# Packed attention and a two-layer mixer on one core: the packed values as twenty small matmuls instead of five wide ones

## The chip, the core and the metric

The kernel runs on one core of a Trainium2 chip. The core has a matrix engine (TensorE, PE; its weight loads are listed apart as PEld), three engines for elementwise work (VectorE or DVE, ScalarE or ACT, GpSimd or POOL), a sync engine (SyncE, SP) that only issues transfers here, and 16 DMA engines that move data between the device memory and the on-chip memory. Matrix products land in PSUM, a small accumulator memory of 128 partitions, and are read from there by DVE or ACT.

The metric is device microseconds from the first to the last instruction of one execution, as the runs report it. Lower is better. Before the change three runs gave 883.6, 884.82 and 885.3 us; the median is 884.82 us.

## The reference, cut to what matters

```python
# batch 8, heads 8, seq 576, head_dim 64, 32 packs; q, k, v, p in float32
def sm_attn(qq, kk, vv):
    s = scale * np.matmul(qq, kk.transpose(0, 1, 3, 2))
    s = s - np.max(s, axis=-1, keepdims=True)
    a = np.exp(s)
    a = a / (np.sum(a, axis=-1, keepdims=True) + 1e-09)
    return np.matmul(a, vv)
p_packed = sm_attn(p, k, v)                  # per batch and head: [32, 64]
x = sm_attn(q, p_packed, p_packed)           # heads side by side: [8, 576, 512]
h = x.transpose(0, 2, 1) @ U @ V             # mixes tokens, rank 32
u = x + h.transpose(0, 2, 1)
out = u + np.maximum(u @ w_ch1, 0.0) @ w_ch2 # 512 -> 2048 -> 512
```

U, V, w_ch1 and w_ch2 arrive as float64 and are made float32 on the chip.

## The kernel before, in words

The work has two phases. Phase A makes the packed values `pp` of every batch, which is `p_packed` of the reference, and the product `pp w1` for the first four batches. Phase B computes, batch by batch, the two large products, while the attention of the next batches and `pp w1` of the later ones are made beside it.

In phase A the unit of work is four heads of one batch: 16 units, u = 0 to 15. A unit goes through these steps. `a_load` and `a_load_v` bring k and v. `a_split` transposes k on DVE (tile `kT`, one instruction at line 106). `a_scores` makes the scores of the 4 x 32 packs against 576 tokens on PE (line 331), so that partition 32 h + n of the tile `s_ps` is pack n of head h. `a_softmax` takes the row maximum on DVE (line 339, tile `mx`) and the exponential on ACT (line 341). `a_turn` transposes the exponentials back on PE (lines 351 and 352) and copies them on ACT into `eT`, five blocks of up to 128 tokens, the last of 64. `a_pack` multiplies them with v (lines 367 and 368, tile `pp_ps`) and scales the result on ACT into `ppall` (line 371). `a_pairs` transposes pairs of heads for the product with w1.

In `a_pack` before the change the left operand is a block of `eT` with all four heads' 32 packs as its 128 columns, and the right operand is v of all four heads, 4 x 64 columns. The product therefore holds every head's packs against every head's values, 128 x 256, of which the four blocks on the diagonal are used. Each block is read by a copy of its own, 32 partitions by 64.

Between the units phase A converts w1, 16 chunks of 128 x 512. One conversion is a square on ACT (line 67), four instructions on DVE (lines 68, 69, 70 and 76), a rounding copy on ACT (line 128, tile `w1h`) and a subtraction on POOL (line 129, tile `w1l`). `fold(r, pr)` multiplies the transposed packed values of round r (two batches) with the four chunks of row block pr of w1 (tile `w_ps`, three buffers; three matmuls a chunk, lines 81 to 83), copies each chunk's product to a tile `fold` (six buffers; line 401 on ACT, and in round 1 line 399 on DVE for every second chunk) and writes it to device memory (line 402, target `wsr`). The folds take their `fold` tiles in the order of the program, all of round 0 before round 1, so the 16 folds of round 1 come after the one that needs the last chunk of w1. `load_wt` reads the first columns back (line 450), and line 461 on ACT with line 462 on POOL splits them into the tile `wt`, the first weights of phase B.

The attention of batch 0 runs within phase A too, in small steps. Its last ones, which I call the attention's tail, are `tokens` (PE transposes, line 236 on ACT, three subtractions into `tl` at line 237 on DVE), `mix1` (15 matmuls into `m_ps`, line 246 on ACT, two subtractions into `ms` at line 249 on DVE) and `mix2` (four matmuls, four additions into `aT` at line 259 on DVE, line 260 on ACT, line 261 on POOL).

The order in which phase A's instructions stand on each engine isn't that of the source. A scheduler sets it when the program is built: it takes the dependences and its own estimate of every instruction's length, and places what can run. If an instruction is said to be shorter, the order of everything around it can change, on all engines and in the DMA queue of SP. An engine then executes its instructions strictly in that fixed order, and waits where an operand is late. Phase B is in an order written out by hand.

Of the kernel before, what the change touches and what calls it, by code (L numbers as in the profile page):

```python
# [8 lines left out]
F32 = mybir.dt.float32  # L9
# [10 lines left out]
def packed_attention_mixer_kernel(  # L20
# [11 lines left out]
):  # L32
    """x = packed attention, u = x + (x^T U V)^T, out = u + relu(u w1) w2.

    The attention output has rank 32 per head: x = A pp with A [tokens, (head, pack)].  So
    u = A' pp with A' = A + (A^T U V)^T, and u w1 = A' (pp w1).  Phase A makes pp of every batch and
    pp w1 of the first half of them; phase B does the rest of each batch while A' of the next one and
    pp w1 of the later ones are made.

    The large products are of float32r: an operand is the exact sum of two such parts (hi, lo), a  # L40
    product is hi*hi + hi*lo + lo*hi.  U, V, w1 and w2 come as the bits of float64 and are made
    float32 on the chip, to all 24 bits.
    """
    nc = tc.nc
    B, H, S, D = q.shape
# [11 lines left out]
    HALF = ((0, 256), (256, 320))  # L57
    # the float32 with the bits of the high word of the float64 2^-126
    LEAST = 1.125 * 2.0 ** -15
# [3 lines left out]
    def float32_of(x, t, raw, pool):  # L63
        """x (int32 words) = float32 bits of the float64s in raw [..., 2]; t is as large.  A float64
        below float32's normal range becomes zero, on GpSimd if pool."""
        low, high = raw[:, :, 0], raw[:, :, 1]
# [27 lines left out]
    nc.gpsimd.memset(bdq, 0.0)  # L94
    # pp w1: rows (pair of heads, batch of a round, head, pack) of the first batches, (head, pack) of the others
    wsr = [dram.tile([2 * H * NP, DF], F32, name=f"wsr{r}", tag=f"wsr{r}") for r in range(2)]
    wsc = {b: dram.tile([H * NP, DF], F32, name=f"wsc{b}", tag=f"wsc{b}") for b in range(B // 2, B)}

# [1 line left out]
    def load_nat(pool, bufs, src, b, g):  # L100
# [10 lines left out]

# [1 line left out]
    def weight_tiles(name):  # L113
# [16 lines left out]

# [1 line left out]
    uh = const.tile([P, 5, 4, R], F32R, name="uh")  # L132
# [31 lines left out]

# [1 line left out]
    def attention(b, res):  # L166
        """Steps that leave A'^T of batch b, in hi and lo parts, in res."""
        st = {}
# [114 lines left out]

    # ================= phase A: packed keys and values, and pp w1 of the first batches =================
    actx = ExitStack()
# [75 lines left out]
    def a_pack(u):  # L361
        b, g = UN[u]
        eT, vt, rs = ua[u]["eT"], ua[u]["v"], ua[u]["sum"]
        pp_ps = psA.tile([P, 4, D], F32, name="pp_ps", bufs=1)
        vm = vt[:, :4].rearrange("p h x -> p (h x)").rearrange("p (h k d) -> p k h d", h=4, k=4)
        for kk in range(4):
            nc.tensor.matmul(pp_ps, lhsT=eT[:, kk], rhs=vm[:, kk], start=kk == 0, stop=False)
        nc.tensor.matmul(pp_ps, lhsT=eT[:64, 4], rhs=vt[:64, 4].rearrange("p (h d) -> p h d", h=4), start=False, stop=True)
        for h in range(4):
            hs = slice(32 * h, 32 * h + 32)  # L370
            nc.scalar.activation(ppall[hs, b, g], pp_ps[hs, h], AF.Copy, scale=rs[hs])
        if b < B // 2:
            ua[u]["twice"] = sA.tile([P, 2, D], F32, name="twice", bufs=1)
            nc.scalar.copy(ua[u]["twice"], ppall[:, b, g].unsqueeze(1).to_broadcast([P, 2, D]))

    def a_pairs(u):
        """pp^T, block diagonal over the heads of a pair, for the two batches of a round"""
        b, g = UN[u]
# [11 lines left out]
    def fold(r, pr):  # L390
        """rows of pp w1 of a pair of heads, of both batches of round r"""
        wh, wl = w1t[pr]
# [145 lines left out]

    # ================= phase B =================
    ctx.enter_context(tc.manual_schedule())  # L540
# [17 lines left out]

# [1 line left out]
    def later(pr):  # L560
# [50 lines left out]
    class Batch:  # L611
# [8 lines left out]
        def blocks(self):  # L620
            """pp, block diagonal over the heads of a group, and the columns of A' left for the joint tile"""
            for h in range(4):
# [54 lines left out]
    def joint(b):  # L677
        """the last 64 tokens of batches b - 1 and b"""
        oj = psO.tile([P, DM], F32, name="o", tag="o")
        for kt in range(NK):  # L680
            kj = jslot(b, kt)
            mm3(oj, (hjh[:, kj], hjl[:, kj]), w2_parts(kt), kt == 0, kt == NK - 1)
            if kt == 0:
                for i in range(2):
                    residual(oj, ajh[i], ajl[i], rdh[i], rdl[i])
        return oj
# [107 lines left out]
```

## Time and profile before

| | |
|---|---|
| median of three runs | 884.82 us (883.6 to 885.3) |
| profiled execution, first to last instruction | 882.5 us |
| PE busy | 830.5 us, 94% |
| DVE busy | 538.2 us, 61% |
| ACT busy | 374.7 us, 42% |
| POOL busy | 317.7 us, 36% |
| copies of `pp_ps` on ACT, line 371 | 64, 19.5 us |
| matmul passes into `pp_ps`, lines 367 and 368 | 160 |

The profiled execution has a time of its own, 882.5 us between its first and its last instruction; what a run reports beyond that lies around the span. Shares over the whole span hide that the two phases are bound by different engines; a table by stretches of time shows it. In the lists below, a line number is that of the kernel before; "out<-in" names the tiles; "x8" is a count of merged instructions; a bracket behind a row is the idle time before it and what ended it. A float32 matmul is listed as two passes, each with its weight load. The end of a pass is modelled, so the distance between the starts of two passes says more than the length of one.

### The profile page before, as it was taken

Reading aid. Unit: us, or ns where it says so; the run is one execution under the profiler, and the core shown is the slowest. Engines: PE = TensorE matmul, PEld = TensorE weight load, DVE = VectorE, ACT = ScalarE, POOL = GpSimd, SP = SyncE. Lnnn points to the kernel's source line nnn. Section 1 sums busy time; section 2 is a strip of 40 time slices with the busy share of each in tenths; the row PEclk is TensorE's granted clock in tenths of the full one; section 3 lists DMA queues with packets and bytes.
Section 4 is the critical chain, followed back from the end, with each engine's and each line's share of the span. In section 5 each row is a group of like instructions: output and inputs, shape, how many; then the busy total and the mean of one; then the engine's idle time right before and its main releaser. Section 6 shows DMA issues by size and latency. Waiting matters only on the chain.

```text
span 882.5 us, 12689 instructions
## 1 busy us (share of the span) xinstructions
PE 830.5 (94%) x4480; PEld 708.8 (80%) x4480; DVE 538.2 (61%) x1023; ACT 374.7 (42%) x960; POOL 317.7 (36%) x268
## 2 busy tenths in 40 slices
PE   4889788878989999999999999999999999999997
PEld 3556566767879888898889888988898889889886
DVE  7999997989957876478676343444543524432220
ACT  2556567634444555455554233223333322333220
POOL 3322344745346545255454232323232313221110
PEclk9999899999999999999999999999999999999999
DMA  9879657723424444334452203010301120002001
GB/s 315 239 241 289 208 174 256 256 79 103 157 63 121 130 141 124 113 102 120 128 166 87 65 13 111 25 43 34 111 25 56 55 76 25 25 13 93 28 1 59
DMA packets 59998, 98.55 MB, mean 112 GB/s; under 512 B 12192, under 2 KB 36768, under 8 KB 59936
## 3 DMA queue, kind: packets, MB, share of 16 engines
q1 hardware_dynamic: 59936, 97.75, 35.2%
q8 instruction: 35, 0.57, 0.3%
q14 instruction: 27, 0.22, 0.1%
HBM read 71.52 MB, written 26.21 MB: 111 GB/s over the span
## 4 chain that ended last, share of the span: by engine, by line
PE 68%; DVE 21%; issue 4%; POOL 2%; DMA 2%; ACT 2%; SPq 0%; DVEq 0%; ACTq 0%
PE o L83 14%; PE o L81 13%; PE o L82 13%; PE h_ps L81 7%; PE h_ps L82 6%; PE h_ps L83 6%; DVE os L69 3%; DVE kT L106 3%; DVE os L70 2%; DVE natT L106 2%; DVE os L76 2%; DVE os L68 2%; PE w_ps L601 2%; DVE hl L649 1%; PE t_ps L234 1%
## 5 line engine op out<-in xcount | busy, mean ns | idle before, releaser
L649 DVE SCALAR_TENSOR_TENSOR hl<-h_ps,hh 128x256 fp32r<-128x256 f32 x256 | 104.1, 418 | 180.8 <-ACT hh L647 145.0
L83 PE MATMUL o<-w2h,hl 128*128 128x512 f32 x512 | 202.0, 395 | 0.0
L81 PE MATMUL o<-w2h,hh 128*128 128x512 f32 x512 | 201.1, 393 | 0.0
L82 PE MATMUL o<-w2l,hh 128*128 128x512 f32 x512 | 200.7, 392 | 0.0
L647 ACT ACTIVATE hh<-h_ps 128x256 fp32r<-128x256 f32 x256 | 96.0, 384 | 231.4 <-PE h_ps L83 228.4
L462 POOL TENSOR_TENSOR fold<-fold 128x512 fp32r<-128x512 f32 x62 | 83.6, 1349 | 217.2 <-ACT fold L461 216.5
L81 PE MATMUL h_ps<-ah,fold 128*128 128x256 f32 x496 | 149.4, 301 | 10.2 <-DVE hl L649 9.8
L82 PE MATMUL h_ps<-al,fold 128*128 128x256 f32 x496 | 146.3, 295 | 0.0
L83 PE MATMUL h_ps<-ah,fold 128*128 128x256 f32 x496 | 145.7, 294 | 0.0
L83 PEld LDWEIGHTS o<-w2h,hl 128*128 128x128 f32 x512 | 96.3, 188 | 21.4
L82 PEld LDWEIGHTS o<-w2l,hh 128*128 128x128 f32 x512 | 96.5, 189 | 17.6
L81 PEld LDWEIGHTS o<-w2h,hh 128*128 128x128 f32 x512 | 96.4, 188 | 16.8
L81 PEld LDWEIGHTS h_ps<-ah,fold 128*128 128x128 f32 x496 | 93.4, 188 | 17.8 <-DVE hl L649 14.6
L82 PEld LDWEIGHTS h_ps<-al,fold 128*128 128x128 f32 x496 | 93.5, 189 | 2.2
L83 PEld LDWEIGHTS h_ps<-ah,fold 128*128 128x128 f32 x496 | 93.5, 188 | 0.0
L190 POOL TENSOR_TENSOR nlo<-natT,nhi 128x576 fp32r<-128x576 f32 x32 | 46.7, 1476 | 106.9 <-ACT nhi L189 106.9
L69 DVE SCALAR_TENSOR_TENSOR os<-bits,os 128x512 int32<-128x512 int32 x48 | 55.9, 1164 | 1.3
L331 PE MATMUL s_ps<-kT,bdp 128*128 128x288 f32 x128 | 42.4, 485 | 10.7 <-DVE bdp L322 8.9
L70 DVE SCALAR_TENSOR_TENSOR os<-bits,os 128x512 int32<-128x512 int32 x48 | 45.2, 943 | 1.5
L331 PEld LDWEIGHTS s_ps<-kT,bdp 128*128 128x128 f32 x128 | 28.4, 230 | 20.0 <-issue 8.9
L189 ACT CAST nhi<-natT 128x576 fp32r<-128x576 f32 x32 | 20.7, 674 | 54.7 <-DVE natT L106 52.0
L129 POOL TENSOR_TENSOR w1l<-os,w1h 128x512 fp32r<-128x512 f32 x16 | 21.9, 1366 | 57.6 <-ACT w1h L128 57.6
(148 smaller groups left out, 1472.3 us busy)
## 6 DMA issues: line engine op xcount, KB each, us to landing
bits<-in_moe_w_ch_dram SPq DMA_DIRECT2D x48, 512.0 KB, 4.2
nat<-in_k_dram SPq DMA_DIRECT2D x16, 576.0 KB, 4.9
nat<-in_q_dram SPq DMA_DIRECT2D x16, 576.0 KB, 4.4
vt<-in_v_dram SPq DMA_DIRECT2D x16, 512.0 KB, 5.8
wsr<-fold SPq DMA_DIRECT2D x32, 256.0 KB, 4.3
out_dram<-bits SPq DMA_DIRECT2D x16, 512.0 KB, 3.0
wsc<-bits SPq DMA_DIRECT2D x64, 128.0 KB, 2.2
fold<-wsc SPq DMA_DIRECT2D x32, 256.0 KB, 2.7
```

Of the source, the lines that this page charges most:

```text
L69: nc.vector.scalar_tensor_tensor(x, high, -0x40000000, x, op0=ALU.bitwise_and, op1=ALU.bitwise_or)
L70: nc.vector.scalar_tensor_tensor(x, low, 29, x, op0=ALU.logical_shift_right, op1=ALU.bitwise_or)
L81: nc.tensor.matmul(ps, lhsT=lh, rhs=rh, start=start, stop=False)
L82: nc.tensor.matmul(ps, lhsT=lh, rhs=rl, start=False, stop=False)
L83: nc.tensor.matmul(ps, lhsT=ll, rhs=rh, start=False, stop=stop)
L106: nc.vector.transpose(t.rearrange("p h (i c) -> p c h i", c=NB), nat.rearrange("p (c h l) -> p c h l", h=2, l=32),)
L129: nc.gpsimd.tensor_tensor(lo, x, hi.bitcast(F32), op=ALU.subtract)
L190: nc.gpsimd.tensor_tensor(lo[:, dh], t, hi[:, dh].bitcast(F32), op=ALU.subtract)
L331: nc.tensor.matmul(s_ps[:, hf, :288], lhsT=bdp[b % 2][:, 2 * g + dh], rhs=kT[:, dh, 288 * hf:288 * hf + 288], start=dh == 0, stop=dh == 1)
L462: nc.gpsimd.tensor_tensor(lo, raw, hi.bitcast(F32), op=ALU.subtract)
L647: nc.scalar.activation(hi, src, AF.Relu)
L649: nc.vector.scalar_tensor_tensor(lo, src, 0.0, hi.bitcast(F32), op0=ALU.max, op1=ALU.subtract)
```

## The change

`pp_ps` shrinks from 128 x 256 to 128 x 64. For each of the five blocks of tokens four small matmuls take one head each: the 32 columns of that head in `eT` against the 64 columns of that head's v. Each writes the 32 partitions of its head, so the four of a block fall into four column tiles of the array. One scaled copy on ACT then takes all 128 partitions, with each partition's own scale. The comments become blank lines, and one line is added in `a_pack`, so line numbers behind 371 are higher by one in the changed kernel: its folds are copied at lines 400 and 402, written at 403, read back at 451 and split at 462 and 463.

```diff
     def a_pack(u):
         b, g = UN[u]
         eT, vt, rs = ua[u]["eT"], ua[u]["v"], ua[u]["sum"]
-        pp_ps = psA.tile([P, 4, D], F32, name="pp_ps", bufs=1)
+        pp_ps = psA.tile([P, D], F32, name="pp_ps", bufs=1)
         vm = vt[:, :4].rearrange("p h x -> p (h x)").rearrange("p (h k d) -> p k h d", h=4, k=4)
-        for kk in range(4):
-            nc.tensor.matmul(pp_ps, lhsT=eT[:, kk], rhs=vm[:, kk], start=kk == 0, stop=False)
-        nc.tensor.matmul(pp_ps, lhsT=eT[:64, 4], rhs=vt[:64, 4].rearrange("p (h d) -> p h d", h=4), start=False, stop=True)
-        for h in range(4):
-            hs = slice(32 * h, 32 * h + 32)
-            nc.scalar.activation(ppall[hs, b, g], pp_ps[hs, h], AF.Copy, scale=rs[hs])
+        for kk in range(5):
+            rows = P if kk < 4 else 64
+            for h in range(4):
+                hs = slice(32 * h, 32 * h + 32)
+                rhs = vm[:, kk, h] if kk < 4 else vt[:rows, 4, D * h:D * h + D]
+                nc.tensor.matmul(pp_ps[hs], lhsT=eT[:rows, kk, hs], rhs=rhs, start=kk == 0, stop=kk == 4)
+        nc.scalar.activation(ppall[:, b, g], pp_ps, AF.Copy, scale=rs)
         if b < B // 2:
```

The first place is PE in phase A, around one unit's `pp_ps`: - is before, + the change.

```order
 L331 MATMUL s_ps<-kT,bdp_97 128x288 x4
-L367 MATMUL pp_ps<-vt,eT 128x256 x4
-L368 MATMUL pp_ps<-vt,eT 128x256
+L371 MATMUL pp_ps<-vt,eT 32x64 x20
 L351 MATMUL t_ps<-ident,e_180 128x128 x4
```

Five matmuls of 256 columns become twenty of 64, in the same place; nothing else moves here.

The second place is DVE late in phase A, around the last conversions of w1. Four rows L68, L69, L70, L76 are one conversion; `tl`, `ms` and `aT` (but not the transpose at line 222) are the attention's tail; `fold` is a copy of round 1. Before:

```order
L68 TENSOR_SCALAR os<-bits 128x512
L69 SCALAR_TENSOR_TENSOR os<-bits,os 128x512
L70 SCALAR_TENSOR_TENSOR os<-bits,os 128x512
L76 SCALAR_TENSOR_TENSOR os<-os 128x512
L237 TENSOR_TENSOR tl<-t_ps,th 128x512 x2
L237 TENSOR_TENSOR tl<-t_ps,th 64x256
L399 COPY fold<-w_ps 128x512
L249 TENSOR_TENSOR ms<-m_ps,ms 32x256 x2
L399 COPY fold<-w_ps 128x512
L68 TENSOR_SCALAR os<-bits 128x512
L259 TENSOR_TENSOR aT_1053<-v_ps,aT_1053 128x288
L259 TENSOR_TENSOR aT_1308<-v_ps,aT_1308 128x288
```

The first four rows of this piece are the last conversion of w1. In the changed kernel the same conversion stands at the end of the piece, ahead of the fold:

```order
L259 TENSOR_TENSOR aT_1173<-v_ps,aT_1173 128x288
L259 TENSOR_TENSOR aT_1464<-v_ps,aT_1464 128x288
L76 SCALAR_TENSOR_TENSOR os<-os 128x512
L68 TENSOR_SCALAR os<-bits 128x512
L69 SCALAR_TENSOR_TENSOR os<-bits,os 128x512
L70 SCALAR_TENSOR_TENSOR os<-bits,os 128x512
L76 SCALAR_TENSOR_TENSOR os<-os 128x512
L68 TENSOR_SCALAR os<-bits 128x512
L69 SCALAR_TENSOR_TENSOR os<-bits,os 128x512
L70 SCALAR_TENSOR_TENSOR os<-bits,os 128x512
L76 SCALAR_TENSOR_TENSOR os<-os 128x512
L400 COPY fold<-w_ps 128x512
```

All nine instructions of the attention's tail now stand ahead of the last conversion of w1; no other DVE instruction has crossed it in either direction.

The third place is ACT at the same time, around the two splits `wt`. Before:

```order
L67 ACTIVATE os<-bits 128x512
L401 COPY fold<-w_ps 128x512 x2
L461 CAST wt_1461<-os 128x512
L246 CAST ms<-m_ps 128x256
L461 CAST wt_1464<-os 128x512
L401 COPY fold<-w_ps 128x512 x2
```

And in the changed kernel:

```order
L128 CAST w1h_95<-os 128x512
L402 COPY fold<-w_ps 128x512
L67 ACTIVATE os<-bits 128x512
L462 CAST wt_1653<-os 128x512
L462 CAST wt_1656<-os 128x512
L402 COPY fold<-w_ps 128x512 x2
```

Before, the copies of the last fold of round 0 and the first of round 1 stand ahead of the two splits; in the changed kernel they stand behind both, and nine copies of folds follow the splits, where before there were seven. In SP's queue the four reads that feed the splits (line 450, now 451) stand, before and now, behind the load of the second chunk of w2, which takes the buffer that the last conversion of w1 gives free at line 70.

## The prediction

> **What bounds the kernel now.** I read the page's span, then a table of stretches of time, because busy shares of the whole span mix two phases, and then the list of DVE's waits.
>
> ```profile
> span 882.5 us, 12689 instructions
> ...
> core 0: us, PE busy (x) PEld busy (x) DVE busy (x) ACT busy (x) POOL busy (x), PEclk, DMA share, GB/s
> 6.00:142.00 136.00, 111.98 (x451) 80.84 (x451) 132.90 (x219) 79.79 (x207) 44.77 (x40) 0.92 0.78 248
> 142.00:164.00 22.00, 18.87 (x90) 14.12 (x90) 17.05 (x29) 13.99 (x33) 13.92 (x17) 1.00 0.83 265
> 164.00:242.00 78.00, 68.45 (x382) 59.39 (x383) 73.42 (x119) 34.41 (x83) 36.39 (x26) 0.98 0.39 132
> 242.00:882.00 640.00, 631.24 (x3559) 554.47 (x3557) 314.18 (x661) 245.18 (x639) 218.18 (x172) 1.00 0.24 74
> ```
>
> The columns behind the window are PE, PEld, DVE, ACT and POOL. From 242 us on PE is busy 631.24 of 640 us: that stage is PE's, and the change isn't in it. From 6 to 142 us, the stage in which the change lies, DVE is busy 132.90 of 136 us, PE 111.98, ACT 79.79. DVE sets the pace there, and keeps it to 242 us (73.42 of 78). The list of waits says the same more sharply: from 0 to 142 us DVE has one wait, for the first k. The only stretch in which DVE waits at all before phase B is 142 to 164 us:
>
> ```profile
> DVE kT L106 <- DMA nat<-in_k_dram: 5.4, 1, 5.4
> ...
> DVE ms L249 <- ACT ms L246: 1.7, 1, 1.7
> DVE tl L237 <- ACT th L236: 1.3, 1, 1.3
> DVE fold L399 <- PE w_ps L83: 1.2, 1, 1.2
> DVE fold L399 <- ACT fold L401: 0.4, 1, 0.4
> ```
>
> So time is to be won or lost at two places: where DVE's order is changed, and where PE would become slower than DVE. DVE stays close to full until PE takes over at about 242 us, so I take a delay of DVE's last work of phase A (a fold copy, which ends at 163.70, below) one to one into the end.
>
> **The parts: matmuls.** One unit before, in order of time:
>
> ```profile
> 70.74 0.63 PE L351 MATMUL t_ps<-ident,e 128*128 128x128 f32 x4
> ...
> 71.21 1.89 PE L367 MATMUL pp_ps<-vt,eT 128*128 128x256 f32 x8
> 73.03 0.29 PEld L368 LDWEIGHTS pp_ps<-vt,eT 64*128 64x128 f32 x2 [0.33 <-issue]
> 73.03 0.70 PE L368 MATMUL pp_ps<-vt,eT 64*128 64x256 f32 x2
> 73.66 0.11 PEld L352 LDWEIGHTS t_ps<-ident,e 128*64 128x64 f32 x1 [0.33 <-ACT e L341]
> 73.66 0.30 PE L352 MATMUL t_ps<-ident,e 128*64 128x128 f32 x1
> ```
>
> The ten passes last from 71.21 to 73.73, 2.52 us, 0.25 us a pass of 256 columns. The changed unit has 20 matmuls, so 40 passes of 64 columns and 32 weight columns. No row shows such a pass. Bounds: if time goes with the columns, a pass is a quarter, 0.063 us, and 40 are 2.52 us, as before. If the four heads of a block run side by side in their column tiles, a quarter of that, 0.63 us. If a small pass cannot start sooner after the last one than the smallest passes here do, it is L351's step: four passes in 0.63, one lasts 0.30, so three steps in 0.33, 0.11 us; 40 are 4.4 us. I take 2.5 us: L352's load of 64 weight columns lasts 0.11 us and L368's two of 128 together 0.29, so size matters, and nothing here shows two passes at once. PE's own sum is then nothing. Its cover is 136 - 112 = 24 us of idle PE beside DVE's work; at the upper end 16 x 1.9 = 30 us more would outgrow it by 6 us.
>
> [...]
>
> **The parts: copies.** The four copies of 32 x 64 become one of 128 x 64, of the same 64 columns:
>
> ```profile
> L371 ACT ACTIVATE ppall<-pp_ps,sm 32x64 f32<-32x64 f32 x64 | 19.5, 305 | 1.1 <-PE pp_ps L368 0.3
> ```
>
> 48 of 64 go: 48 x 0.305 = 14.6 us less on ACT. ACT is busy 79.79 of 136 us there, and DVE waits for it nowhere up to 142 us, so I book nothing. Bounds from nothing to the 1.3 us that `tl` waits for ACT later.
>
> **The parts: DVE's order.** This is where I see a price. The scheduler now puts the nine instructions of the attention's tail ahead of the last conversion of w1, and leaves the folds of round 1, which need that conversion, behind. The rows before:
>
> ```profile
> 141.32 0.69 DVE L70 SCALAR_TENSOR_TENSOR os<-bits,os 128x512 int32<-128x512 int32 x1
> 141.41 1.72 POOL L129 TENSOR_TENSOR w1l<-os,w1h 128x512 fp32r<-128x512 f32 x1 [3.38 <-ACT w1h L128]
> 142.12 1.56 DVE L76 SCALAR_TENSOR_TENSOR os<-os 128x512 f32<-128x512 f32 x1
> 143.61 1.28 DVE L237 TENSOR_TENSOR tl<-t_ps,th 128x512 fp32r<-128x512 f32 x2
> 143.75 1.92 SPq L450 DMA_DIRECT2D os<-wsr  x3
> 146.21 0.42 DVE L237 TENSOR_TENSOR tl<-t_ps,th 64x256 fp32r<-64x256 f32 x1 [1.33 <-ACT th L236]
> 146.35 0.58 SPq L450 DMA_DIRECT2D os<-wsr  x1
> 149.26 0.63 ACT L461 CAST wt<-os 128x512 fp32r<-128x512 f32 x1
> 150.20 0.86 DVE L249 TENSOR_TENSOR ms<-m_ps,ms 32x256 fp32r<-32x256 f32 x2 [1.67 <-ACT ms L246]
> 150.59 0.62 ACT L461 CAST wt<-os 128x512 fp32r<-128x512 f32 x1 [0.41 <-DMA os<-wsr]
> 152.55 0.39 PE L81 MATMUL w_ps<-w1h,lwh 128*128 128x512 f32 x1
> 152.77 0.81 DVE L259 TENSOR_TENSOR aT<-v_ps,aT 128x288 f32<-128x288 f32 x2
> 153.23 0.39 PE L81 MATMUL w_ps<-w1h,lwh 128*128 128x512 f32 x1
> 155.91 0.81 DVE L259 TENSOR_TENSOR aT<-v_ps,aT 128x288 f32<-128x288 f32 x2
> 162.36 0.59 ACT L401 COPY fold<-w_ps 128x512 f32<-128x512 f32 x1 [1.07 <-DMA wsr<-fold]
> 163.00 0.69 DVE L399 COPY fold<-w_ps 128x512 f32<-128x512 f32 x1 [0.41 <-ACT fold L401]
> ```
>
> Step one: the nine cost 1.28 + 0.42 + 0.86 + 0.81 + 0.81 = 4.18 us of DVE. DVE has no idle time ahead of that point, so L70 of the last conversion, which ended at 142.01, ends at 146.2. If `tl` and `ms` wait there as they do now, it's up to 3.0 us later still; conversions now stand between them, so I book none.
>
> Step two: from that L70 to the last fold copy. Before, 163.70 - 142.01 = 21.7 us. In the changed order ACT's copy of the last fold of round 0 stands behind both splits `wt`, and these wait for the reads at line 450, which SP issues only after that L70. Behind the splits in ACT's queue are nine fold copies; PE waits for them with its three `w_ps` buffers, and DVE waits with its own copy for PE. The second split ended 151.21 - 142.01 = 9.2 us after L70, and I keep that. Then one copy, 0.59 us. Then 14 of the 16 folds of round 1 are still to be made (two fit in the free buffers). PE needs 153.23 - 152.55 = 0.68 us for one; 14 x 0.68 and a last copy of 0.69 is 10.2 us. As they went before, the 14 copies on ACT and DVE behind the second split took 163.70 - 151.21 = 12.5 us, 0.89 us each, held up by the landing of `fold` writes (the bracket at 162.36). So step two is 9.2 + 0.59 + 10.2 = 20.0 at least, 22.3 at most; against 21.7 that is -1.7 to +0.6. Between them I take the middle, -0.6.
>
> The sum is 4.2 - 0.6 = 3.6 us later, bounds 2.5 to 4.8, and 7.8 with the waits of step one. The conversions can shift it either way, as they often run beside POOL's large subtractions:
>
> ```profile
> L69 DVE SCALAR_TENSOR_TENSOR os<-bits,os 128x512 int32<-128x512 int32 x18 | 18.9, 1052 | 0.2
> ```
>
> L69 has a mean of 1.05 us up to 164 us, but its like, L70 at 141.32, took 0.69; L76 at 142.12 took 1.56 beside L129 on POOL. Which ones coincide is a matter of order. Eighteen conversions with 0.9 us for each hit more or less: I allow two hits, 1.8 us, either way. The rest of the kernel, 163.70 to the end, is in the order written by hand, and I leave it unchanged.
>
> The span becomes 882.5 + 3.6 = 886.1 us. The median of the runs stands 884.82 - 882.5 = 2.3 us above the span; the predicted time is 888.4 us.
>
> **Rivals.** First, no change: DVE's sum of work is the same, and the fold stage could take back what step one costs, if PE's bound of 20.0 us holds and the second split comes some 2 us sooner, since on ACT nothing of `ms` stands between the splits now. For it: the split at 150.59 waited 0.41 us for its read only. Against it: the last copies waited for the landing of writes, and these are closer together now. Time 882.5 + 4.2 - 3.7 + 2.3 = 885.3 us.
>
> Second, faster: DVE's waits between 142 and 164 us, 1.7 + 1.3 + 1.2 + 0.4 = 4.6 us, all vanish. The first two can, since conversions fill them. For the two of the folds PE and ACT would have to be ahead of DVE, with 14.6 us less on ACT. Against it stands ACT's queue with the splits ahead. Time 884.8 - 4.6 = 880.2 us.
>
> Third, slower by more: PE becomes the bound in the units. It decides once a unit's passes cost over 2.5 + 24/16 = 4.0 us. [...] DVE would then wait at `mx`, line 339, in most units. [...]
>
> Fourth, the change doesn't do what it says: the four column tiles run one after another. That is the price I took, and costs nothing while DVE is the bound; it isn't counted apart.
>
> **How the numbers follow.** Forecast 0.48, with a range of its own of 886.5 to 891; no change 0.24; faster 0.18; PE as the bound 0.10. A measurement of this kernel can tell about 0.2%, 1.8 us, from no change; so slower than that is 0.48 + 0.10 = 0.58, the same 0.24, faster 0.18. The predicted time is the forecast's, 888.4 us. For 8 in 10 the range takes in the case without change, the upper bound with the waits of step one (884.8 + 7.8 = 892.6) and one hit more of 0.9 us, and the less lucky half of the faster case: 881.0 to 893.5 us.
>
> **What would show it.** Right: the last L76 of a w1 conversion ends near 148 us where it was 143.68; the last fold copy on DVE ends near 167 instead of 163.70; in between DVE waits some 6 us for `fold`, ACT for `wt`; the stretch up to 142 us has DVE without waits, and ACT's copies of `ppall` are 16 of about 0.3 us. Wrong: DVE waits for PE at `mx` (the third rival); the last fold copy ends at or ahead of 163.70 (the first two); or the difference lies behind 164 us, where I booked nothing.

## The result, and the profile after

The changed kernel takes 898.14 us (median of four runs, 897.6 to 899.85) where the kernel before takes 884.26 us beside it. The ratio is 1.0159, interval 1.0145 to 1.0174: 13.9 us slower. I had predicted 888.4 us, at most 893.5.

The same stretches of time as in the prediction, now of the changed kernel (its copy of `ppall` is line 372):

```profile
core 0: us, PE busy (x) PEld busy (x) DVE busy (x) ACT busy (x) POOL busy (x), PEclk, DMA share, GB/s
6.00:142.00 136.00, 97.93 (x948) 69.14 (x948) 129.91 (x219) 65.24 (x162) 43.67 (x39) 0.86 0.78 239
142.00:164.00 22.00, 12.91 (x31) 8.08 (x30) 13.92 (x16) 9.75 (x19) 10.36 (x9) 0.60 0.59 188
164.00:242.00 78.00, 66.05 (x343) 56.20 (x342) 70.32 (x107) 33.61 (x79) 35.36 (x32) 0.93 0.44 143
```

ACT is busy 14.5 us less up to 142 us, as the edit says, and PE 14 us less, though TensorE's granted clock is lower there, 0.86 instead of 0.92. But from 142 to 164 us every engine does less than it did: PE 12.91 us instead of 18.87, DVE 13.92 instead of 17.05, and the clock is 0.60 where it was 1.00. The list of DVE's waits up to 180 us has grown from five rows to ten:

```profile
DVE kT L106 <- DMA nat<-in_k_dram: 5.6, 1, 5.6
DVE fold L400 <- PE w_ps L83: 4.2, 4, 1.5
DVE fold L400 <- DMA os<-wsr: 4.1, 1, 4.1
DVE mx L339 <- PE s_ps L331: 1.5, 2, 1.1
DVE os L68 <- POOL wt L463: 1.1, 1, 1.1
DVE tl L237 <- PE pp_ps L371: 1.1, 1, 1.1
DVE lwl L389 <- ACT lwh L388: 0.7, 1, 0.7
...
DVE aT L259 <- PE v_ps L258: 0.5, 1, 0.5
```

In order of time on DVE, from the last conversion of w1 to the last fold copy:

```profile
148.42 0.43 DVE L68 TENSOR_SCALAR os<-bits 128x512 int32<-128x512 int32 x1
...
149.61 1.64 DVE L70 SCALAR_TENSOR_TENSOR os<-bits,os 128x512 int32<-128x512 int32 x1
151.35 0.69 DVE L76 SCALAR_TENSOR_TENSOR os<-os 128x512 f32<-128x512 f32 x1
156.14 0.69 DVE L400 COPY fold<-w_ps 128x512 f32<-128x512 f32 x1 [4.10 <-DMA os<-wsr]
...
164.61 4.28 DVE L68 TENSOR_SCALAR os<-bits 128x512 int32<-128x512 int32 x1
168.93 0.69 DVE L69 SCALAR_TENSOR_TENSOR os<-bits,os 128x512 int32<-128x512 int32 x1
169.54 0.68 DVE L400 COPY fold<-w_ps 128x512 f32<-128x512 f32 x1
...
173.74 0.69 DVE L400 COPY fold<-w_ps 128x512 f32<-128x512 f32 x1 [1.53 <-PE w_ps L83]
175.12 0.69 DVE L400 COPY fold<-w_ps 128x512 f32<-128x512 f32 x1 [0.69 <-PE w_ps L83]
176.49 0.69 DVE L400 COPY fold<-w_ps 128x512 f32<-128x512 f32 x1 [0.68 <-PE w_ps L83]
```

The last conversion of w1 ends at 152.04 us (143.68 before), the last fold copy at 177.18 (163.70 before), 13.5 us later. The profiled span is 896.8 us, 14.3 more than before. So the loss lies where I had looked for it, between the units and the end of the folds; behind that only 0.8 us are added. One row stands out: the L68 at 164.61 lasts 4.28 us, where the one at 148.42 lasts 0.43. On POOL at that time:

```profile
164.44 1.30 POOL L129 TENSOR_TENSOR w2l<-os,w2h 128x512 fp32r<-128x512 f32 x1 [4.18 <-ACT w2h L128]
165.67 1.00 POOL L558 MEMSET rdh<- 128x512 f32 x2
166.60 1.00 POOL L558 MEMSET rdl<- 128x512 f32 x2
167.53 0.58 POOL L558 MEMSET ajh<- 128x256 f32 x2
168.04 0.58 POOL L558 MEMSET ajl<- 128x256 f32 x2
```

L68 starts beside the subtraction L129, which eight clearings follow without a pause until 168.62, and ends 0.27 us behind the last of them. And PE's clock shows in the spacing of the fold passes:

```profile
154.62 0.63 PE L81 MATMUL w_ps<-w1h,lwh 128*128 128x512 f32 x1
155.04 0.63 PE L82 MATMUL w_ps<-w1l,lwh 128*128 128x512 f32 x1
...
159.31 0.65 PE L81 MATMUL w_ps<-w1h,lwh 128*128 128x512 f32 x1 [2.69 <-ACT fold L402]
159.75 0.63 PE L82 MATMUL w_ps<-w1l,lwh 128*128 128x512 f32 x1
...
163.75 0.40 PE L81 MATMUL w_ps<-w1h,lwh 128*128 128x512 f32 x1
163.98 0.39 PE L82 MATMUL w_ps<-w1l,lwh 128*128 128x512 f32 x1
```

0.42 to 0.44 us lie between two passes at 154 and 159 us, 0.23 at 163.75. A table by 3 us shows a clock of 0.50 in five rows one after another, from 141 to 156 us:

```profile
141.00:144.00 3.00, 1.31 (x4) 0.68 (x3) 2.44 (x5) 2.43 (x7) 2.68 (x3) 0.50 0.50 122
144.00:147.00 3.00, 0.80 (x1) 0.29 (x1) 2.93 (x3) 0.38 (x1) 2.99 (x3) 0.50 0.38 143
147.00:150.00 3.00, 2.01 (x3) 0.79 (x3) 2.74 (x5) 1.80 (x3) 0.94 (x1) 0.50 0.43 150
150.00:153.00 3.00, 1.48 (x3) 0.76 (x4) 1.94 (x2) 0.93 (x2) 0.93 (x2) 0.50 0.46 164
153.00:156.00 3.00, 3.00 (x8) 2.32 (x9) 0.00 (x0) 0.88 (x3) 1.04 (x1) 0.50 0.91 307
```

The trace shows the clock fall and come back: 1.00 from 135 to 138 us, 0.67 in the next 3 us, then 0.50 up to and with the first row in which PE is busy throughout, and 0.98 in the 3 us behind it. A row without any work is not there: PE is busy 0.80 to 2.01 us in each of the four rows before, and no wait of PE between 137 and 156 us is longer than 2.12 us. How much idle time goes with a fall of the clock is therefore open here.

Three explanations were to be told apart. **The order**: the scheduler's new order of phase A costs the time, whatever the small matmuls cost. **The idle PE**: the small matmuls themselves leave PE idle, the clock falls, and the passes behind take twice as long. **The run on POOL**: the L68 behind the clearings costs some 4 us.

### The profile page after: what moved, and what is told of

Same layout as the page of the kernel before. It is cut to its first block, busy times and chain, and to the rows that moved or that the text cites. A ratio compares the mean times of both kernels' runs of the same rounds, so it can differ in the third digit from the quotient of the medians.

```text
span 896.8 us, 13590 instructions
## 1 busy us (share of the span) xinstructions
PE 822.0 (92%) x4960; PEld 700.8 (78%) x4960; DVE 542.2 (60%) x1023; ACT 361.0 (40%) x912; POOL 318.1 (35%) x268
## 4 chain that ended last, share of the span: by engine, by line
PE 67%; DVE 10%; issue 2%; ACT 2%; POOL 2%; DMA 1%; SPq 0%; DVEq 0%; ACTq 0%; POOLq 0%
PE o L83 14%; PE o L82 13%; PE o L81 13%; PE h_ps L81 7%; PE h_ps L82 6%; PE h_ps L83 6%; DVE os L69 2%; PE w_ps L602 2%; DVE os L68 1%; DVE os L70 1%; DVE natT L106 1%; DVE hl L650 1%; DVE os L76 1%; PE t_ps L234 1%; DMA bits<-in_moe_w_ch_dram 1%
## 5 line engine op out<-in xcount | busy, mean ns | idle before, releaser
L81 PEld LDWEIGHTS h_ps<-ah,fold 128*128 128x128 f32 x496 | 93.6, 189 | 16.6 <-DVE hl L650 13.5
L69 DVE SCALAR_TENSOR_TENSOR os<-bits,os 128x512 int32<-128x512 int32 x48 | 53.6, 1118 | 1.4
L70 DVE SCALAR_TENSOR_TENSOR os<-bits,os 128x512 int32<-128x512 int32 x48 | 49.9, 1040 | 1.3
L129 POOL TENSOR_TENSOR w1l<-os,w1h 128x512 fp32r<-128x512 f32 x16 | 21.8, 1363 | 56.1 <-ACT w1h L128 56.1
```

The costliest lines, as they stand in the source:

```text
L69: nc.vector.scalar_tensor_tensor(x, high, -0x40000000, x, op0=ALU.bitwise_and, op1=ALU.bitwise_or)
L70: nc.vector.scalar_tensor_tensor(x, low, 29, x, op0=ALU.logical_shift_right, op1=ALU.bitwise_or)
L81: nc.tensor.matmul(ps, lhsT=lh, rhs=rh, start=start, stop=False)
L129: nc.gpsimd.tensor_tensor(lo, x, hi.bitcast(F32), op=ALU.subtract)
```

## Experiments: order against matmuls

The scheduler's choice can be overruled. A table at the end of the kernel lists the instructions of phase A engine by engine, and each is tied to the one ahead of it in its row (an edge that sets the order of issue and waits for nothing):

```diff
-    actx.close()
+    in_order(tc, nc); actx.close()
...
+def in_order(tc, nc):
+    """Each engine's instructions of phase A in the order of the table."""
+    made = {i.name: i for i in nc.cur_bb.bb.instructions}
+    how = mybir.DependencyInfo(mybir.DependencyClass.NoSync, mybir.DependencyReason.DATA)
+    for row in ORDER:
+        for x, y in zip(row, row[1:]):
+            tc.add_manual_dep(made[f"I-{y}"], f"I-{x}", how, reason="order")
```

So both kernels can be run in both orders. The small matmuls and the one copy in the order of the kernel before (the twenty matmuls stand where the five stood, the copy where the last of the four stood):

> The changed kernel with its 20 small matmuls and one copy a unit, but with the order of every engine's instructions in phase A tied to that of the kernel before. Order theory (the 13.9 us come from the scheduler's new order alone): 883 to 886 us, the last DVE fold copy ends near 164. Idle-PE theory (the small matmuls leave PE idle, the granted clock falls, the s_ps and w_ps passes take twice as long): PE idles as much in this order, so most of the loss stays, 892 us or more, and the clock from 142 to 164 us is well below 1.

Measured: 885.63 us, ratio 1.0012 (1.0001 to 1.0022). And the wide passes and four copies in the order of the changed kernel:

> The kernel before with its ten wide passes and four copies a unit, but with the order of every engine in phase A tied to that of the changed kernel. Order theory: 896 to 899 us, the last L70 of a w1 conversion ends near 151 and the last DVE fold copy near 177, with a low clock in between, since the folds lack their last w1 whatever the small matmuls cost. Idle-PE theory: 884 to 890 us, with the clock near 1 from 142 to 164 us.

Measured: 903.77 us, ratio 1.0210 (1.0189 to 1.0231), above the 896 to 899 us of the order theory and far from the other's 884 to 890. The stretch in question, first of the small matmuls in the old order, then of the wide ones in the new order (columns as above):

```profile
142.00:164.00 22.00, 19.50 (x88) 14.81 (x89) 16.07 (x26) 12.31 (x27) 13.44 (x16) 0.92 0.79 251
```

```profile
142.00:164.00 22.00, 11.72 (x28) 6.24 (x27) 15.99 (x22) 8.98 (x18) 10.98 (x9) 0.63 0.55 168
```

The order decides. In the old order the change costs 0.2% at most; in the new order the kernel is slow with either kind of matmul, and with the wide ones slower by 5.6 us than with the small ones. DVE then waits more in the units, for ACT: 3.5 us at `lwl` instead of 0.7, and 2.5 at `sm`, where none is listed for the changed kernel; whether the wide passes or the four copies bring these was not tried. The low clock goes with the order as well: 0.63 with the wide passes. That is against the idle PE as a cause of its own: with the wide passes PE idles there too. In the old order the small matmuls do empty PE (the clock is 0.85 up to 142 us, 0.92 from 142 to 164), and DVE waits 3.0 us for the first fold instead of 1.2, but the whole costs 1.2 us.

In the table, "last w1" is the end of the last L76 of w1, "split" that of the second split `wt` on ACT, "fold" that of the last fold copy on DVE, all from the order of time in the profiles, in us. The last rows are told below.

| kernel | median | last w1 | split | fold | span |
|---|---|---|---|---|---|
| before | 884.26 | 143.68 | 151.21 | 163.70 | 882.5 |
| changed | 898.14 | 152.04 | 158.77 | 177.18 | 896.8 |
| small matmuls, old order | 885.63 | 143.66 | 151.62 | 164.61 | 883.3 |
| wide matmuls, new order | 903.77 | 158.06 | 164.79 | 184.35 | 902.9 |
| changed, tail put behind | 889.10 | 146.12 | 156.13 | 169.15 | 887.3 |
| before, tail put ahead | 897.11 | 155.63 | 161.68 | 175.58 | 895.4 |
| small matmuls, four copies | 891.08 | 148.86 | 154.93 | 168.47 | 887.0 |
| changed, PE kept busy | 894.18 | 151.24 | 158.38 | 173.54 | 893.2 |
| changed, clearings moved | 895.40 | 152.01 | 159.34 | 173.59 | 893.5 |
| changed, both | 894.56 | 151.52 | 158.87 | 173.25 | 893.0 |

Which part of the order is it? The prediction named the attention's tail. One edge alone, `tl` behind the last L76 of w1, in the changed kernel (`kept` holds the instructions of line 76 as they are made, w1's sixteen first):

```diff
+            kept.append(nc.vector.scalar_tensor_tensor(xf, t, ...))
...
+            tail = nc.vector.tensor_tensor(tl[:rows, ks], ...)
+            b or tc.add_manual_dep(tail.ins, kept[15].ins.name, NOSYNC, reason="order")
```

> The changed kernel with one order put in by hand: the attention's tail (the first tl on DVE) may not stand ahead of the last conversion of w1; what follows from it is left to the scheduler, everything ahead of the tail stands as in the changed kernel. Theory of the tail (the tail ahead of the last conversions is the part of the new order that costs): 883 to 887 us, the last L76 of w1 near 144 and the last DVE fold copy near 164. Rival (the loss is in the other rearrangements of the units up to 130 us, waits at mx and lwl): 893 us or more.

Measured: 889.10 us, ratio 1.0054 (1.0037 to 1.0071). Of the 13.9 us 9.0 are won back, less than the theory's 11 or more, and more than the rival's 5. The low clock isn't gone with the tail: it is 0.50 in every row of 3 us from 138 to 150 us, and 0.77 from 142 to 164. DVE's waits of this kernel:

```profile
DVE ms L249 <- ACT ms L246: 4.5, 1, 4.5
DVE fold L400 <- PE w_ps L83: 2.2, 1, 2.2
DVE mx L339 <- PE s_ps L331: 1.3, 2, 1.0
DVE lwl L389 <- ACT lwh L388: 0.6, 1, 0.6
```

The other way round, the kernel before with its tail where the changed kernel has it (a chain over the tail and the two conversions around it, on DVE alone):

> The kernel before, with its wide passes and four copies, and one order put in by hand: the nine DVE instructions of the attention's tail stand between the last conversions of w1 as they do in the changed kernel. Theory of the tail: the last L76 of w1 comes 5 to 9 us later than 143.7, the stretch up to 160 us has a clock near 0.6, the time is 893 to 900 us. Rival (the tail's place alone costs only its own 4.2 us or less): 885 to 889 us.

Measured: 897.11 us, ratio 1.0146 (1.0131 to 1.0161), with a clock of 0.56 from 142 to 164 us. Nine instructions of 4.18 us, moved ahead, make the kernel before slower by 12.6 us, without a single small matmul. Its L68 near 164 us took 0.43 us, so the run on POOL has no part in that. That this is nearly the whole loss is in part chance, for it isn't made up as in the changed kernel. Here the first `tl` waits 5.7 us for PE, where it waited 1.1 us there, and two steps of the attention ahead of it wait another 3.1 us (1.8 for ACT, 1.3 for POOL):

```profile
137.65 1.29 DVE L237 TENSOR_TENSOR tl<-t_ps,th 128x512 fp32r<-128x512 f32 x2 [5.66 <-PE pp_ps L368]
```

So the run shows that the tail's place, with what the scheduler makes of it, can cost this much, and not that it does so in the changed kernel; for that the 9.0 us of the run before stand.

And the small matmuls with the four copies kept, in whatever order the scheduler gives them:

> The small matmuls alone, with four copies a unit as before, in the order that the scheduler makes of it: the attention's tail stands ahead of the last conversions there too. Theory of the tail: 895 to 903 us, as the changed kernel or a little later; the copies change nothing by themselves. Rival (it is the lighter ACT that makes the difference): within 2 us of the kernel before.

Measured: 891.08 us, ratio 1.0073 (1.0053 to 1.0094). Here I missed. The tail stands ahead of the last conversions there too, so the matmuls alone turn the scheduler's order; the one copy alone was not tried. But this is a third order, in which the last w1 ends at 148.86 and no L68 stands behind the clearings. Having the tail ahead does not have one price: how much DVE waits on the way depends on where its pieces fall.

## Experiments: the clock and the run on POOL

PE kept busy: in the changed kernel's own order, passes that nobody reads are put at the places where PE waits.

```diff
-        pp_ps = psA.tile([P, D], F32, name="pp_ps", bufs=1)
+        pp_ps = psA.tile([P, 512], F32, name="pp_ps", bufs=1)[:, :D]
...
+    idle = psA.tile([P, 512], F32, name="pp_ps", bufs=1)
+    dead = [nc.tensor.matmul(idle, lhsT=vs[:, :P], rhs=vs[:, :512], start=True, stop=True).ins.name for _ in range(49)]
+    in_order(tc, nc, dead); actx.close()
```

> The changed kernel in its own order, with 49 more passes of 512 columns on PE into the idle pp_ps bank, which nobody reads, in the places between 137 and 170 us where PE waits: work is added, none left out. Theory of the clock (PE idles, the granted clock falls to 0.5, and the fold passes behind take 0.43 us instead of 0.23): clock 0.95 or more from 142 to 164 us, fold passes 0.23 us apart, 2 to 3.5 us won, 894.5 to 896 us. Rival (the slow passes are not on the path; DVE, ACT's wt splits and the L68 of 4.28 us set the end): 897.5 to 899 us, or later by the passes themselves.

Measured: 894.18 us, ratio 1.0111 (1.0094 to 1.0128), 4.0 us less than the changed kernel, with more work on PE, and a little more than the theory's 2 to 3.5. In its profile the clock is 1.00 and the fold passes follow at 0.23 us:

```profile
142.00:164.00 22.00, 16.27 (x64) 11.22 (x63) 15.12 (x17) 10.21 (x19) 12.06 (x11) 1.00 0.61 187
```

So the clock is part of the price of the new order. The clearings, moved to just ahead of the batch that uses them, four at a time:

```diff
-    for t in (*rdh, *rdl, *ajh, *ajl):
-        nc.gpsimd.memset(t.bitcast(F32), 0.0)
...
+            if b < 2 and kt == 1:
+                [nc.gpsimd.memset(x[b].bitcast(F32), 0.0) for x in (rdh, rdl, ajh, ajl)]
```

> The changed kernel in its own order; only the eight clearings of rdh, rdl, ajh and ajl on POOL, which run in a row at the start of phase B, are made four at a time just before the batch that uses them. Theory of the POOL run (the one L68 of 4.28 us at 164.6 stands behind w2l and these clearings): that L68 takes about 0.4 us, the last fold copy comes 3 to 4 us sooner, 894 to 895 us. Rival (that L68 is not on the path, or it meets the next POOL instruction): 897.5 to 898.5 us.

Measured: 895.40 us, ratio 1.0119 (1.0101 to 1.0137): 2.7 us won of the 3 to 4 expected. The L68 there still meets L129 on POOL, but nothing behind it:

```profile
164.98 1.46 DVE L68 TENSOR_SCALAR os<-bits 128x512 int32<-128x512 int32 x1
```

```profile
164.86 1.30 POOL L129 TENSOR_TENSOR w2l<-os,w2h 128x512 fp32r<-128x512 f32 x1 [3.96 <-ACT w2h L128]
```

It is not a cure in general. The same move with the small matmuls in the old order:

> The small matmuls and the one copy in the order of the kernel before (as the first kernel of this set), with the clearings moved as in the third. If order is the cause and the clearings cost something in that order too: 880 to 884 us, faster than the kernel before. If the clearings only hurt in the changed order: the same as the first kernel of this set, within 1 us.

Measured: 888.80 us, ratio 1.0038 (1.0025 to 1.0051), 3.2 us slower than without it. In the old order the clearings met L70, L76 and fold copies, which kept their usual 0.68 to 1.67 us; moved, they met an L68, which then took 2.15 us. That L68 isn't all of it: it starts at 173.53 us, and the last fold copy had ended 1.7 us later already (166.31 instead of 164.61), behind a wait of 4.2 us for the first fold instead of 3.0. Why that wait is longer was not tried, and the result is as neither theory had it.

Do the two gains add up? With both edits:

> The changed kernel in its own order with both cures at once: the 49 unread passes that keep PE busy between 137 and 170 us, and the eight clearings moved to the batches that use them. Theory (the loss of 13.9 us is three parts: the tail's place with its waits, the low clock, the L68 behind POOL's run): the gains of 4.0 and 2.7 us add up, 891 to 892 us, L68 near 0.4 us and the clock 0.95 or more from 142 to 164 us; what remains, 7 us, is the tail's 4.2 us and its waits. Rival (the two overlap, since both shorten the same folds): 893.5 us or more.

Measured: 893.71 us, ratio 1.0107 (1.0078 to 1.0137), but its four runs are 890.70, 892.46, 894.95 and 898.26 us. The profiled one is the slowest of them; it had a clock of 0.57 from 162 to 165 us and an L68 of 1.85 us beside the moved clearings. Two runs lie near the theory and two with the rival, so nothing follows from it. A better form leaves the clearings in a row, puts them ahead of w2l on POOL, and has 55 unread passes:

```diff
-    split_w2(*convert_w2(0))
+    w2first = convert_w2(0)
...
     for t in (*rdh, *rdl, *ajh, *ajl):
         nc.gpsimd.memset(t.bitcast(F32), 0.0)
+    split_w2(*w2first)
```

> The changed kernel in its own order, with 55 unread passes at the places where PE waits, and with the eight clearings left in a row but put ahead of w2l on POOL (w2h and w2l of the first tile of w2 come behind them). Theory of three parts: the clearings run near 161 to 164 us beside copies and L70, which they do not hold up, L68 near 164 us no longer stands behind a run, and both gains add up: 890.5 to 892 us; 7 us are left for the tail's own 4.2 us and its waits. Rival (the gains overlap): 893.5 to 895 us.

Measured: 894.56 us, ratio 1.0108 (1.0093 to 1.0123). The clock is 1.00, and the L68 takes 0.66 us:

```profile
162.49 0.66 DVE L68 TENSOR_SCALAR os<-bits 128x512 int32<-128x512 int32 x1
...
167.19 0.69 DVE L400 COPY fold<-w_ps 128x512 f32<-128x512 f32 x1 [0.82 <-DMA wsr<-fold]
169.35 0.69 DVE L400 COPY fold<-w_ps 128x512 f32<-128x512 f32 x1 [1.47 <-PE w_ps L83]
171.18 0.69 DVE L400 COPY fold<-w_ps 128x512 f32<-128x512 f32 x1 [1.14 <-PE w_ps L83]
```

Both causes are gone, and the gain is that of one: in this form the rival was right, they overlap. The two runs near 891 us above leave open whether they always do. A link between the two stands in the trace of the changed kernel. The long L68 holds up a fold copy, PE stands idle behind that copy for 3.61 us, and the clock, full from 165 to 168 us, is 0.64 again from 171 to 174:

```profile
170.27 0.79 PE L81 MATMUL w_ps<-w1h,lwh 128*128 128x512 f32 x1 [3.61 <-DVE fold L400]
```

From the second split to the last fold copy this kernel takes 14.4 us, the one with the clearings moved 14.3, the one with PE kept busy 15.2, the changed kernel 18.4, the kernel before 12.5. About 14.3 us stay in both kernels without the long L68. In this order the folds of round 1 nearly all come behind the splits, and their copies then wait for PE and for the landing of `fold` writes, as the rows show; which of these sets the pace was not tried.

## Experiments: what the small matmuls are worth

The loop over heads outside, so that the passes of one column tile follow each other, in the old order:

```diff
-        for kk in range(5):
-            rows = P if kk < 4 else 64
-            for h in range(4):
-                hs = slice(32 * h, 32 * h + 32)
+        for h in range(4):
+            hs = slice(32 * h, 32 * h + 32)
+            for kk in range(5):
+                rows = P if kk < 4 else 64
```

> The small matmuls and the one copy in the order of the kernel before, but inside a unit the loop over heads is outside: the five passes of one column tile follow each other, so that no two tiles can run side by side. If the gain on PE is from four tiles at a time: the 20 matmuls of a unit take 2 to 2.6 us on PE, as the wide ones did, instead of 0.55 us. If small passes are as quick by themselves: about 0.6 us. In both cases the time is that of the first kernel of the first set, within 2 us, since DVE is the bound there.

Measured: 884.84 us, ratio 1.0005 (0.9994 to 1.0015). A unit's 40 passes in the changed kernel, and then with the heads outside:

```profile
20.39 0.90 PE L371 MATMUL pp_ps<-vt,eT 128*32 128x64 f32 x40
```

```profile
19.93 3.23 PE L371 MATMUL pp_ps<-vt,eT 128*32 128x64 f32 x40
```

From the first start to the last end it is 0.90 us with four column tiles in turn, 3.23 with one after another, and 2.52 for the ten wide passes. So the gain on PE is that of four tiles side by side. And in the old order it is worth nothing: with the slower loop PE is busy 118.73 us up to 142 us instead of 98.00, the clock from 142 to 164 us is 1.00 instead of 0.92, and the time is 0.8 us lower rather than higher, with intervals that overlap. The 3.23 us are more than the 2 to 2.6 I expected; a part is the changes between blocks of 128 and 64 rows, seven a unit now, of some 0.09 us each (below).

If DVE is the bound, work taken from DVE must pay. ACT has 14.6 us more, so it takes over four casts:

```diff
-            nc.vector.tensor_copy(uh[:n, ks], src)
+            nc.scalar.copy(uh[:n, ks], src)
...
-            nc.vector.tensor_copy(vs[:, cs], vx)
+            nc.scalar.copy(vs[:, cs], vx)
...
-        nc.vector.tensor_scalar_add(sm, sm, 1e-9)
```

> The small matmuls and the one copy in the order of the kernel before, and with the time that ACT has won put to use: the four casts of uh and vs go from DVE to ACT (1.3 us), and DVE no longer adds 1e-9 to the 16 sums sm (2.2 us; a sum holds exp(0), so that it is about 1 or more, where the addition changes no bit). Theory (DVE is full up to 142 us and sets the end one to one): 3.5 us ahead of the first kernel of the first set, 881.5 to 882.5 us. Rival (transfers or the fold stage behind set the end): 884 to 886 us.

Measured: 883.49 us, ratio 0.9988 (0.9979 to 0.9998), 2.1 us less than without it, where 3.5 were expected. With unread passes near 140 us:

> As the kernel with the lighter DVE, and with 11 unread passes on PE at the two places near 140 us where it waits for the last split of w1, behind which the clock was 0.59 from 144 to 147 us in this order. Clock theory: DVE's wait of 3.0 us for the first fold falls to about 1.5 us, 880 to 881.5 us. Rival (that wait is made up for by the work behind it): as the kernel without these passes, within 0.5 us.

Measured: 887.49 us, ratio 1.0033 (1.0021 to 1.0046): slower. The passes go into the tile of `pp_ps`, and near 140 us that is not free yet, so that they brought a wait of their own ahead of the folds:

```profile
142.16 2.93 PE L538 MATMUL pp_ps<-vs 128*128 128x512 f32 x6 [4.97 <-ACT ppall L371]
```

The heads outside keep PE busy without that:

> The kernel with the lighter DVE, small matmuls, one copy and the old order, with the loop over heads outside, so that PE is kept longer at the units. Clock theory: the stretch from 142 to 164 us is granted 0.98 or more, DVE's wait for the first fold falls from 3.4 to about 2 us, 882 to 883 us. Rival (the clock does not matter in this order): 883.5 us, as with the heads inside.

Measured: 883.08 us, ratio 0.9988 (0.9976 to 1.0000). The clock is 1.00 from 142 to 164 us; the gain over the heads inside, 0.4 us, can't be told from none. And the control, the lighter DVE in the kernel before:

> The kernel before, with its wide passes and four copies in its own order, and only the lighter DVE (casts of uh and vs on ACT, no 1e-9 added to the 16 sums). If the small matmuls and the one copy give nothing in this order: the same as the kernel with both, 882.5 to 884 us. If ACT's 14.6 us are needed to take over the casts, or the lighter PE to keep pace: 884.5 us, no gain over the kernel before.

Measured: 882.86 us, ratio 0.9979 (0.9970 to 0.9988). This is the lowest median of all, though 883.08 and 883.49 can't be told from it, and it has no part of the change: the wide matmuls leave room enough on PE, and the four copies on ACT.

## Why the prediction was wrong

The direction, the place and the carrier of most of the loss (9.0 us of 13.9) were right: DVE's order, the attention's tail ahead of the last conversions, the end of the folds. The size was a quarter of it, 3.6 us of 13.9. Two terms failed: step one, which booked no waits (9.2 us instead of 4.2), and step two, which priced the folds at a full clock and without a stop (25.9 us instead of 20.0 to 22.3). The two are 9.2 us and 25.9 - 21.7 = 4.2 us later than before, which is the delay of the last fold copy, 13.5 us.

**The parts: matmuls.** I took 2.5 us a unit, the price by columns; it is 0.90 where nothing comes between the passes, near the lower bound of 0.63; 2.52 to 0.90 is 2.8 times. "PE's own sum is then nothing" holds in the old order (1.0012). Where the rows go from 128 to 64, the weight load at L368 had stood idle 0.33 us before (the bracket in the prediction's rows). What such a change costs PE is less: with the heads outside, the starts of two passes across a change from 128 to 64 rows or back lie 0.15 us apart and others 0.06 (single passes in the trace), so it costs about 0.09 us there; before, the first pass of L368 starts 0.31 us behind the last of L367, whose own lie 0.22 apart. The entry into the column tiles costs as little: from the last pass of `s_ps` to the first of `pp_ps` it is 0.34 us between starts in the changed kernel and 0.24 before.

**The parts: copies.** As said there: 16 copies of 0.31 us, and nothing gained, since the lighter DVE is as quick with the four copies (882.86 us) as with the one (883.49).

```profile
L372 ACT ACTIVATE ppall<-pp_ps,sm 128x64 f32<-128x64 f32 x16 | 5.0, 313 | 4.4 <-PE pp_ps L371 4.2
```

**DVE's order, step one** put the last conversion 4.2 us later and booked no waits, since "conversions now stand between them"; 3.0 us of waits were the bound. Measured on L70: 151.25 - 142.01 = 9.2 us. The tail's own 4.18 us are in it, and waits, which did come: `tl` 1.1 and `aT` 0.5 us, within the bound I had set aside. What I had not seen is `mx` 1.5 and `lwl` 0.7 us in the units, where the prediction said "DVE without waits": the new order of the units itself. With that L70's own 0.95 us more (1.64 instead of 0.69, beside POOL) this makes 8.9 of the 9.2 us. Putting the tail behind leaves the waits in the units (1.3 and 0.6), and the last w1 still ends 2.4 us late.

**Step two**, from that L70 to the last fold copy, was to take 20.0 to 22.3 us and took 177.18 - 151.25 = 25.9. Its first piece was shorter than I took it: the second split came 7.5 us behind L70, not the 9.2 that I kept. The second piece failed: "PE needs 153.23 - 152.55 = 0.68 us for one" is a price at a clock of 1.00, read in a stretch in which PE was busy. The new order emptied that stretch (PE is busy 12.91 us instead of 18.87 from 142 to 164 us, at a clock of 0.60); at a clock of 0.50, with 0.42 to 0.44 us between passes, the three passes of a fold take 1.3 us. Without the long L68, with PE kept busy, or with both, step two measures 22.4 to 23.1 us, at and just above my upper bound.

**"Two hits, 1.8 us, either way"** was the allowance for DVE beside POOL. One L68 alone took 3.9 us more than usual (4.28 instead of 0.43). The conversions' L69, L70 and L76, which the allowance was taken from, lose about 1 us beside one subtraction of POOL (L70 1.64 us instead of 0.69); L68 is another kind of instruction (TENSOR_SCALAR in the rows, where L69, L70 and L76 are SCALAR_TENSOR_TENSOR), and it met a run of nine.

**The rest after the last fold copy**, left unchanged, is 0.8 us longer; that held.

**The rivals.** PE as the bound did not come: DVE's waits at `mx` are 1.5 us in all, and a unit's 40 passes cost 0.90 us at a full clock (1.45 in the one at 90.16 us, at 0.50), far from the 4.0 at which that rival decides. No change is what the old order gives (885.63 us), and not by the way of that rival, for there nothing is lost that the folds would have to take back. Faster came in no run of the change alone.

The causes, by the runs: the new order of phase A is the loss (898.14 us in it, 885.63 in the old one). Within it, the tail ahead of the last conversions is worth 9.0 us taken away from the changed kernel, with all that follows from it; the 12.6 us put into the kernel before came by other waits. The low clock and the L68 are worth 4.0 and 2.7 us when taken away alone, and 3.6 together in one form. How much of the two lies within the tail's 9.0 isn't shown: with the tail behind, the long L68 is gone (1.47 us at 170.19, behind the last fold copy), but the clock is still 0.50 from 138 to 150 us. That kernel is left 4.5 us slower than the kernel before (889.10 against 884.56 beside it). Waits of 1.9 us in the units and a wait for `ms` that is 4.5 us instead of 1.7 are seen there; what would become of the time without them was not tried.

## What to carry to other kernels

Where a scheduler sets the order from estimated lengths, an edit that makes one engine faster is first of all a new order on all of them; run the edit in the old order and the old code in the new order before the edit gets the blame or the credit. A duration read from the trace of before holds only while its surroundings do: if a move empties PE for some microseconds, the matmuls behind it may have to be priced at half the clock (here 0.43 us between passes instead of 0.23), and an L68 moved next to a run of POOL work at up to that run's length (here 4.28 us instead of 0.43). Two changes of the same size need not have the same cause: the tail moved ahead in the old code cost nearly what the new order did, and DVE waited in other places. Faster work on an engine that isn't the bound was worth nothing here (0.90 or 3.23 us a unit, no difference clear of noise), while 3.5 us taken from the engine that is gave 2.

## What the runs showed of the hardware

**L68 beside POOL.** In six kernels an L68 began while POOL's subtraction L129 was under way and clearings, or nothing, followed. In each it ended 0.27 to 0.29 us behind the last of them: L129 alone 1.46 us (clearings moved), four clearings 2.15 and 1.85 us, eight 4.28, 4.40 and 4.42 us. L70, L76 and the fold copies beside the same clearings kept to their 0.7 us, or to what they take beside L129 (1.67 us for the L70 at 159.52 us of the kernel before). So an L68 that had started beside the first of nine POOL instructions ended behind the last of them. That isn't always so. In the kernel before, where the subtraction `nlo` follows L129 without a pause, the L68 at 164.74 us took 1.54 us and was done 0.29 us behind L129. And in the kernel with the clearings ahead of w2l an L68 that began amid the clearings took 0.66 us: it ended 0.28 us behind the two `ajh`, and it was the next clearings that took longer (the two `ajl` 0.84 us instead of 0.58):

```profile
162.30 0.57 POOL L560 MEMSET ajh<- 128x256 f32 x2
162.81 0.84 POOL L560 MEMSET ajl<- 128x256 f32 x2
```

What decides which of the two takes longer was not tried, and no run shows why L68 is held up and the others are not.

**Four column tiles start 6 to 7 ns apart.** In the trace of the small matmuls in the old order the single passes of a unit begin at 0, 7, 14 and 20 ns, and each next group of four mostly 56 ns behind the start of the one before; with the heads outside each pass mostly begins 56 ns behind the one before. A group of four costs what one pass costs, 56 ns.

**A few tens of unread passes can hold the clock**, but not in each run: with 49 of them it was 1.00 from 142 to 164 us in one profile (PE kept busy) and 0.94 in another (with the clearings moved as well), where the changed kernel has 0.60. The busy time of a row of 3 us doesn't tell the clock: it was 0.50 with PE busy 2.01 us (changed kernel, 147 to 150), and 1.00 with 1.40 (kernel before, 141 to 144) and 1.34 (PE kept busy, 156 to 159).
